# A third product of each gate and value group in blocks of 128, and GpSimd for the weights' sums behind the last scores

## The chip, the core and the metric

The kernel runs on one core of one Trainium2 chip. The time is that of the device for one execution, in microseconds (us), and the figure that counts is the median of the runs. TensorE (PE) does the matmuls, VectorE (DVE), ScalarE (ACT) and GpSimd (POOL) work elementwise, SyncE (SP) issues the transfers. SBUF is the memory on the chip that all engines read, PSUM the banks that matmuls write.

## What is computed

Attention with a threshold, and behind it a feed-forward block with a gate, all in f32. B, H, S, D = 8, 8, 576, 64; the block has 4608 tokens, width 512 and an inner width of 1536.

```python
scores = q @ k.T / sqrt(D)
scores = where(scores >= max(scores) - 0.02, scores, -1e9)
attn = softmax(scores) @ v                      # (B, H, S, D)
x = attn.transpose(0, 2, 1, 3).reshape(4608, 512)
g = x @ w_gate                                  # 512 -> 1536
out = (g * sigmoid(g) * (x @ w_val)) @ w_out    # 1536 -> 512
```

## The kernel before

**Stages.** After the loads and the first batch, scores and attention of the next batches run slot by slot, and the feed-forward products of earlier batches are put between them. The tokens are cut into chunks c = 0 to 8: eight of 512 tokens, one per batch, and chunk 8 with the last 64 tokens of all eight batches. Behind the last scores, from `tail[0] = True` (L1996) on, chunks 7 and 8 are left, with no scores beside them. This stretch is called the tail here.

**Gate and value products.** A chunk needs, for 256 columns of the inner width at a time (a group, g = 0 to 5), the gate and the value of both halves of 256 tokens (t = 0, 1). A Strassen scheme does this by seven products of operand sums in place of eight; each is four matmuls with a 128x128 weight and 256 tokens. The products are p1 to p7, and results are sums of several of them. Class `Group` does it; it accumulates p1 and p2 in bank a (line L993, tile pa), p6, p7 and p4 in bank b (pb), and p5 and p3 in bank e (pe). PE's order is p1 of a group, then p4 of the group before it (L1073, called from L1872), then p5, p2, p6, p3, p7. ACT copies bank a into b ahead of p6 (L1000), copies half of b out after p6 (L1037) and after p7 (L1068).

**Gating.** `Group.finish` (L1041) does it for one half t: ACT's tanh (L1045), DVE's (tanh + 1) x value with the value read from PSUM (L1046, "value factor" in what follows), and a multiplication by the gate, by POOL (line L846) in the slots and by DVE (line L849) in the tail. L846 and L849 are the helpers for every tensor_tensor of POOL and of DVE. Half t = 0 reads the value from bank a and is done after p3, half t = 1 from bank b after p4. The result lies in tile hall.

**The tail's groups.** There `LateGroup` (L1145) does p5 and p3 "nested": each product of 256 blocks is split again into seven products of 128x128 with 128 tokens (L1154), which fill seven quarters of two banks (tiles pe and sc). They need operand sums of their own: of the tokens, four sums of 128x256 per chunk by DVE (`deepen_x`, L1104), and of the weights, four of 128x256 per group by DVE (`deepen_weights` and `four_sums`, L1136 and L1096), made for the next group as soon as its weights have landed. After the product four operations join the quarters (`four_quarters`, L1120): for p5 from copies that ACT puts into SBUF (L1166, L1167), for p3 from PSUM, with one quarter copied by ACT (L1126). L1184 (g1) then adds p3's result to the half gate of t = 0; an L849 adds p5's result for t = 1 (g2).

**Output products.** `Deep` (L1399) does those of a chunk, hall times w_out, again by seven products, and each of them by seven blocks of 128. Its operand sums of 128x384 (`inner_sums`) and of 128x512 (`sum`) are DVE's in the tail. The sums for its first product are put in line during group 4 (L1879), the next ones behind p4 of group 4 (`early`), the rest at the end. Its first product stands ahead of the last group's p4 (`gates_end`), its second behind it.

**Order of the work.** PE's order is written out by hand. That of DVE, ACT, POOL and SP is made by class `Plan` (L28) while the program is built: every job has an assumed duration, its dependencies and a rank; the planner goes along in assumed time and gives each engine the ready job of the lowest rank, with a little patience for rank 0. `pe` puts PE's work at its place and forces what it depends on to be planned first. What the planner has fixed is the order of instructions in each engine's queue; on the chip an instruction waits for those ahead of it in its queue.

**Weights.** From chunk 2 on the weights' sums of each group are read from a store in HBM (sums_hbm) into one of two places, as a part of 1 MB (weights of p1, p2, p5, p6) and one of 768 KB (p4, p3, p7); the second is issued when the group that had the place before is through with p4.

## Time and profile before

| | us |
|---|---|
| median of three runs | 1373.76 (1372.51, 1373.76, 1375.14) |
| the profiled execution, its own time | 1371.38 |
| its span, first to last instruction | 1369.2 |
| what lies around the span | 2.2 |
| PE, DVE, ACT, POOL busy | 1351.0, 1070.9, 875.5, 719.9 |
| the first product of chunk 7, start of the tail | 1156.34 |
| the first product of chunk 8 | 1261.02 |
| the end of the last matmul | 1365.57 |
| POOL's last instruction ends | 1143.2 |

The granted clock of TensorE was 1.000 of full speed over the span. The profiled execution lies 2.4 us below the median of the runs. In the timeline's lines the columns are the start, the time from it to the end, engine, line, operation, output tile, input tiles, shapes and how many instructions the line joins; several matmuls joined in one line end when the last of them is out of the array, so lines overlap by a fraction of a microsecond, and the distance of starts is what a product costs. A bracket at the end is the idle time before it and what ended that. In the groups' lines, the busy sum in us and the mean of one in ns stand behind the first bar, and the idle time before them behind the second.

### The profile page before, as it was taken

The numbers are of one execution on the slowest core, as the hardware profiler recorded it, in microseconds if no ns is written. First come the engines' busy times: TensorE is split into PE (matmuls) and PEld (weight loads), VectorE is DVE, ScalarE is ACT, GpSimd is POOL, SyncE is SP. The second block draws the span as 40 slices with busy tenths as digits, with TensorE's granted clock in tenths as the row PEclk, the third lists the DMA queues.
The fourth block names the chain that finished last, engine by engine and source line by source line (L and its number), as shares of the span: only waits on it lengthen the run. The fifth ranks groups of instructions, "written<-read, shape, count | busy, mean of one in ns | idle before, by whom it ended". The sixth has DMA issues, their size and how long they took to land.

```text
span 1369.2 us, 39187 instructions
## 1 busy us (share of the span) xinstructions
PE 1351.0 (99%) x15590; PEld 1116.1 (82%) x15590; DVE 1070.9 (78%) x2815; ACT 875.5 (64%) x2277; POOL 719.9 (53%) x665
## 2 busy tenths in 40 slices
PE   8999999999999999999999999999999999999998
PEld 7777787778788788877887888877887788999998
DVE  7878888887887777777778777777777776787786
ACT  6888776666756766677776766776767764330330
POOL 2688598663564669434973387427943593000000
PEclk9999999999999999999999999999999999999999
DMA  8752424545525540654154513553165403524411
GB/s 177 200 185 90 82 60 133 146 121 156 151 52 155 144 98 27 181 159 117 37 171 128 150 36 128 144 144 87 36 192 144 113 19 143 162 78 146 151 66 32
DMA packets 208294, 162.32 MB, mean 119 GB/s; under 512 B 166128, under 2 KB 180464, under 8 KB 202736
## 3 DMA queue, kind: packets, MB, share of 16 engines
q1 hardware_dynamic: 203920, 158.86, 41.3%
q8 instruction: 124, 2.03, 0.6%
q10 hardware_dynamic: 4192, 0.95, 0.3%
q14 instruction: 58, 0.48, 0.1%
HBM read 138.28 MB, written 21.50 MB: 117 GB/s over the span
## 4 chain that ended last, share of the span: by engine, by line
PE 90%; DVE 3%; DMA 2%; POOL 2%; SPq 1%; issue 1%; ACT 1%; ACTq 0%; DVEq 0%; POOLq 0%
PE pb L993 18%; PE pa L993 12%; PE px L1473 12%; PE sc L1705 10%; PE pe L993 9%; PE xa L1802 9%; PE po L1269 5%; PE py L1482 5%; PE sc L1154 2%; PE pg L1200 2%; PE pv L1200 2%; PE pe L1154 1%; SPq L367 1%; DMA wo<-in_moe_w_val_dram 1%; PE sc L1473 1%
## 5 line engine op out<-in xcount | busy, mean ns | idle before, releaser
L1753 DVE SCALAR_TENSOR_TENSOR pall<-sc,th,pall 128x288 f32<-128x288 f32 x504 | 244.0, 514 | 65.1 <-ACT pall L1751 50.7
L993 PE MATMUL pb<-xall,big 128*128 128x256 f32 x1152 | 273.5, 380 | 0.0
L1751 ACT ACTIVATE pall<-sc,nm 128x288 f32<-128x288 f32 x504 | 232.2, 498 | 34.1 <-DVE pall L1753 33.8
L993 PEld LDWEIGHTS pb<-xall,big 128*128 128x128 f32 x1152 | 216.4, 190 | 31.0 <-issue 2.2
L1781 DVE STREAM_TRANSPOSE pall<-pall 128x576 f32<-128x576 f32 x252 | 189.7, 765 | 58.2 <-ACT pall L1779 41.4
L1779 ACT ACTIVATE pall<-pall,ri 128x288 f32<-128x288 f32 x415 | 189.8, 529 | 26.3 <-DVE ri L1767 25.8
L846 POOL TENSOR_TENSOR hall<-hall,tmp 128x512 f32<-128x512 f32 x80 | 102.3, 1279 | 159.3 <-DVE hall L1046 141.9
L993 PE MATMUL pa<-xall,big 128*128 128x256 f32 x768 | 183.4, 382 | 0.0
L993 PEld LDWEIGHTS pa<-xall,big 128*128 128x128 f32 x768 | 143.0, 190 | 22.2 <-issue 2.7
L1705 PE MATMUL sc<-kT,qT 64*32 64x144 f32 (+1 forms) x5376 | 150.0, 345 | 2.9 <-DVE pall L1753 1.7
L1726 DVE TENSOR_REDUCE mx<-sc 128x2 f32<-128x576 f32 x168 | 124.8, 743 | 28.6 <-PE sc L1705 28.1
L1705 PEld LDWEIGHTS sc<-kT,qT 64*32 64x32 f32 x5376 | 97.8, 106 | 56.9 <-issue 21.0
L993 PE MATMUL pe<-xall,big 128*128 128x256 f32 x576 | 137.2, 381 | 0.4 <-issue 0.4
L1802 PE MATMUL xa<-pall,vall 64*32 64x288 f32 x4032 | 133.0, 404 | 0.9 <-DVE hall L1046 0.8
L1776 POOL TENSOR_SCALAR pall<-pall,ri 128x288 f32<-128x288 f32 x89 | 88.9, 1010 | 67.0 <-DVE ri L1767 63.8
L993 PEld LDWEIGHTS pe<-xall,big 128*128 128x128 f32 x576 | 108.5, 190 | 17.3 <-issue 2.8
L1802 PEld LDWEIGHTS xa<-pall,vall 64*32 64x32 f32 x4032 | 76.5, 107 | 50.6 <-issue 7.4
L1761 ACT COPY sums<-sums 32x6 f32<-32x6 f32 x336 | 66.8, 199 | 45.6 <-DVE pall L1753 41.1
L1045 ACT ACTIVATE vall<-tmp 128x512 f32<-128x512 f32 x96 | 60.2, 630 | 24.6 <-DVE tmp L1058 9.0
L1482 PE MATMUL py<-wo,hall 128*128 128x256 f32 x336 | 74.8, 379 | 0.0
L1728 DVE TENSOR_REDUCE mx<-sc 128x1 f32<-128x288 f32 x168 | 74.8, 445 | 0.0
L846 POOL TENSOR_TENSOR tmp<-tmp 128x512 f32<-128x512 f32 x36 | 45.9, 1276 | 53.4 <-ACT tmp L1068 53.4
(258 smaller groups left out, 2481.3 us busy)
## 6 DMA issues: line engine op xcount, KB each, us to landing
big<-sums_hbm SPq DMA_DIRECT2D x42, 1024.0 KB, 5.4
big<-sums_hbm SPq DMA_DIRECT2D x48, 768.0 KB, 4.7
vall<-in_v_dram SPq DMA_DIRECT2D x112, 144.0 KB, 3.0
out_dram<-big SPq DMA_DIRECT2D x32, 256.0 KB, 3.0
qT<-in_q_dram SPq DMA_DIRECT2D x112, 72.0 KB, 4.8
kT<-in_k_dram SPq DMA_DIRECT2D x112, 72.0 KB, 3.0
wo<-in_moe_w_gate_dram SPq DMA_DIRECT2D x16, 384.0 KB, 4.1
wo<-in_moe_w_val_dram SPq DMA_DIRECT2D x16, 384.0 KB, 4.8
```

The source lines that it names most:

```text
L846: return lambda: nc.gpsimd.tensor_tensor(out=out, in0=a, in1=b, op=op)
L993: nc.tensor.matmul(ps[:, i], w[:, k_, i * P:(i + 1) * P], x[:, k_, :], start=first and i == k_ == 0, stop=True, skip_group_check=True)
L1473: nc.tensor.matmul(ps, a[:, f, :], ws[n][:, f, :], start=bank_ not in begun, stop=True, skip_group_check=True)
L1482: nc.tensor.matmul(ps(), a[:, f, i * P:(i + 1) * P], operands[o][:, f, :], start=first and f == 0, stop=True, skip_group_check=True)
L1705: nc.tensor.matmul(pss[h][(slice(g * G, (g + 1) * G), *part)], qT[hs, col:col + G], kT[hs, c * SH + keys[0]:c * SH + keys[1]], start=True, ...
L1726: rs.append(job("DVE", 0.72, lambda n=n, tile_=tile_: nc.vector.tensor_reduce(out=mx[:, n:n + 2, 0], in_=tile_[:, :, 0:SH], axis=AX.X, op= ...
L1751: ej = job("ACT", 0.42, lambda x=x, n=n: nc.scalar.activation(ps[x], scs[x], AF.Exp, bias=nm[:, n:n + 1]), ej, *((masks[h, 0], masks[h, 1] ...
L1753: masks[x] = job("DVE", 0.45, lambda x=x, n=n: nc.vector.scalar_tensor_tensor(out=ps[x], in0=scs[x], scalar=th[:, n:n + 1], in1=ps[x], op0 ...
L1776: scaled.append(job("POOL", 1.02, lambda x=x, n=n: nc.gpsimd.tensor_scalar(out=x, in0=x, scalar1=ri[:, n:n + 1], scalar2=None, op0=ALU.mul ...
L1779: scaled.append(job("ACT", 0.46, lambda x=x, n=n: nc.scalar.activation(x, x, AF.Copy, scale=ri[:, n:n + 1]), rj, rank=rank))
L1781: seg["turned"].append(job("DVE", 0.72, lambda both=both: nc.vector.transpose(out=both, in_=both), *scaled, rank=rank))
L1802: nc.tensor.matmul(holds[a].ap()[x * G:(x + 1) * G, 0:SH].rearrange("d (i q) -> d i q", q=G), vr[rs, h, j, ds], p[rs, h, :, j, :], start=( ...
```

## The change

In the tail p4 is done nested, as p5 and p3 are. It writes into two fresh banks rather than onto bank b; ACT copies one quarter, DVE joins the quarters from PSUM, adds bank b (new line L1214), and the value factor of t = 1 then reads its value from SBUF. The weights' sums for the nested products pass from DVE to POOL, and four of 128x128 for p4's weights are added, in turn with the other four. The tokens get four more sums of 128x128 by DVE. The gating multiplication of half t = 0 goes from DVE to POOL, but for group 5. The four sums of 128x384 for product 6 of `Deep` go from DVE to POOL. The lines behind the first edit are shifted by up to 31 in the changed kernel.

```diff
...
-        def finish(self, t, gb, gj, hold, mv):
+        def finish(self, t, gb, gj, hold, mv, y=None):
             n, old = turn_of(n_bufs)
             ht = hall[:, t, self.g]
             rank = 0
             tj = job("ACT", 0.55, lambda: nc.scalar.activation(n.ap, gb.ap, AF.Tanh), gj, *old, rank=rank)
-            vj = job("DVE", 0.7, lambda: nc.vector.scalar_tensor_tensor(out=ht, in0=n.ap, scalar=1.0, in1=hold.rows(), op0=ALU.add,
-                                                                       op1=ALU.mult), tj, mv, rank=rank)
+            vj = job("DVE", 0.7, lambda: nc.vector.scalar_tensor_tensor(out=ht, in0=n.ap, scalar=1.0, in1=hold.rows() if y is None else y,
+                                                                       op0=ALU.add, op1=ALU.mult), tj, mv, rank=rank)
             n.jobs = [vj]
-            hold.read_by(vj)
-            hold.done(True)
-            tt, eng, took = (dve_tt, "DVE", 0.62) if tail[0] else (pool_tt, "POOL", 1.3)
+            if y is None:
+                hold.read_by(vj)
+                hold.done(True)
+            else:
+                e_jobs[0] = [vj]
+            tt, eng, took = (dve_tt, "DVE", 0.62) if tail[0] and (t or self.g == NF2 - 1) else (pool_tt, "POOL", 1.3)
             gated[self.c, t, self.g] = mj = job(eng, took, tt(ht, ht, gb.ap, ALU.mult), vj, rank=rank)
             gb.jobs = [mj]
...
+    w4_places = [x[:, 0:3 * P].rearrange("p (n q) -> p n q", q=P) for x in (tall[:, 4 * HW:], vends.rearrange("p a q -> p (a q)"))]
...
-    def four_sums(places, a11, a12, a21, a22, *deps):
+    def four_sums(took, places, a11, a12, a21, a22, *deps):
 
         p1, p2, p3, p4 = places
-        j1 = job("DVE", 0.36, dve_tt(p1, a21, a22, ALU.add), *deps, rank=1)
-        j2 = job("DVE", 0.36, dve_tt(p2, p1, a11, ALU.subtract), j1, rank=1)
-        j4 = job("DVE", 0.36, dve_tt(p4, a12, p2, ALU.subtract), j2, rank=1)
-        return [j4, job("DVE", 0.36, dve_tt(p3, a11, a21, ALU.subtract), j4, rank=1)]
+        j = job("POOL", took, pool_tt(p1, a21, a22, ALU.add), *deps, rank=1)
+        j = job("POOL", took, pool_tt(p2, p1, a11, ALU.subtract), j, rank=1)
+        j = job("POOL", took, pool_tt(p4, a12, p2, ALU.subtract), j, rank=1)
+        return job("POOL", took, pool_tt(p3, a11, a21, ALU.subtract), j, rank=1)
 
     def deepen_x(c, *deps):
 
         if "t" not in x_deep:
-            x_deep["t"] = [qkp.tile([P, S], F32, name=name)[:, 0:2 * HW // 2].rearrange("p (n o q) -> p n o q", n=2, q=P)
-                           for name in ("qT", "kT")]
-        t12, t34 = x_deep["t"]
+            x_deep["t"] = [qkp.tile([P, S], F32, name=name)[:, 0:HW].rearrange("p (n o q) -> p n o q", n=2, q=P) for name in ("qT", "kT", "qT")]
+        t12, t34, last4 = x_deep["t"]
         x = xall[:, 3 * XW:3 * XW + 3 * HW].rearrange("p (o k n) -> p o k n", o=3, k=2)[:, 0:3:2]
         b11, b12, b21, b22 = (x[:, :, k_, n * P:(n + 1) * P] for k_ in range(2) for n in range(2))
         t1, t2, t3, t4 = t12[:, 0], t12[:, 1], t34[:, 0], t34[:, 1]
-        deps = *ready_x[c][1], *ready_x[c][4], *deps
-        j = job("DVE", 0.36, dve_tt(t1, b12, b11, ALU.subtract), *deps, rank=1)
+        mine = *ready_x[c][1], *ready_x[c][4], *deps
+        j = job("DVE", 0.36, dve_tt(t1, b12, b11, ALU.subtract), *mine, rank=1)
         j = job("DVE", 0.36, dve_tt(t2, b22, t1, ALU.subtract), j, rank=1)
         j = job("DVE", 0.36, dve_tt(t4, b21, t2, ALU.subtract), j, rank=1)
         j = job("DVE", 0.36, dve_tt(t3, b22, b12, ALU.subtract), j, rank=1)
-        x_deep[c] = [j], [(b11[:, o], b21[:, o], b22[:, o], t4[:, o], t1[:, o], t2[:, o], t3[:, o]) for o in range(2)]
+        c11, c12, c21, c22 = (x_block(c, 1, 1)[:, k_, n * P:(n + 1) * P] for k_ in range(2) for n in range(2))
+        u1, u2, u3, u4 = (last4[:, n, o] for n in range(2) for o in range(2))
+        i = job("DVE", 0.23, dve_tt(u1, c12, c11, ALU.subtract), *ready_x[c][0], *deps, rank=2)
+        i = job("DVE", 0.23, dve_tt(u2, c22, u1, ALU.subtract), i, rank=2)
+        i = job("DVE", 0.23, dve_tt(u4, c21, u2, ALU.subtract), i, rank=2)
+        i = job("DVE", 0.23, dve_tt(u3, c22, c12, ALU.subtract), i, rank=2)
+        x_deep[c] = [([j], (b11[:, o], b21[:, o], b22[:, o], t4[:, o], t1[:, o], t2[:, o], t3[:, o])) for o in range(2)]
+        x_deep[c].append(([i], (c11, c21, c22, u4, u1, u2, u3)))
 
     def four_quarters(place, q0, q1, one, *deps, psum=False):
...
 
     def deepen_weights(c, g):
 
-        w = flow[:, g % 2 * GW:(g % 2 + 1) * GW].rearrange("p (o k f) -> p o k f", o=NQ, k=2)[:, 2:6:3]
+        parts_ = flow[:, g % 2 * GW:(g % 2 + 1) * GW].rearrange("p (o k f) -> p o k f", o=NQ, k=2)
+        w, v = parts_[:, 2:6:3], parts_[:, 4]
         a11, a12, a21, a22 = (w[:, :, k_, i * P:(i + 1) * P] for i in range(2) for k_ in range(2))
-        places = [w_place[:, g % 2, n] for n in range(4)]
-        ready = four_sums(places, a11, a12, a21, a22, loads[c, g, 0], loads[c, g, 1], *w_users[g % 2], plan.t + plan.PIPE)
-        s1, s2, s3, s4 = places
-        late_sums[c, g] = ready, [(a11[:, o], a12[:, o], s4[:, o], a22[:, o], s1[:, o], s2[:, o], s3[:, o]) for o in range(2)]
+        v11, v12, v21, v22 = (v[:, k_, i * P:(i + 1) * P] for i in range(2) for k_ in range(2))
+        deps = *w_users[g % 2], plan.t + plan.PIPE
+        s1, s2, s3, s4 = places = [w_place[:, g % 2, n] for n in range(4)]
+        j = four_sums(0.75, places, a11, a12, a21, a22, loads[c, g, 0], loads[c, g, 1], *deps)
+        late_sums[c, g] = [([j], (a11[:, o], a12[:, o], s4[:, o], a22[:, o], s1[:, o], s2[:, o], s3[:, o])) for o in range(2)]
+        u1, u2, u4 = (w4_places[g % 2][:, n] for n in range(3))
+        j = four_sums(0.44, (u1, u2, v21, u4), v11, v12, v21, v22, loads[c, g, 1], *deps)
+        late_sums[c, g].append(([j], (v11, v12, u4, v22, u1, u2, v21)))
 
     class LateGroup(Group):
-        def nested(self, o, first, *deps):
+        def nested(self, o, holds, first, *deps):
-            sums, wd = late_sums[self.c, self.g]
-            ready, xd = x_deep[self.c]
+            sums, wd = late_sums[self.c, self.g][o]
+            ready, xd = x_deep[self.c][o]
 
             def fn():
                 for n in ORDER:
                     b_, at_ = AT[n]
-                    nc.tensor.matmul(self.es[b_].ap()[:, at_ * P:(at_ + 1) * P], wd[o][n], xd[o][n], start=b_ not in begun, stop=True,
+                    nc.tensor.matmul(holds[b_].ap()[:, at_ * P:(at_ + 1) * P], wd[n], xd[n], start=b_ not in begun, stop=True,
                                      skip_group_check=True)
...
         def p5(self):
-            m = self.nested(0, True, *(d for h in self.es for d in h.deps))
+            m = self.nested(0, self.es, True, *(d for h in self.es for d in h.deps))
...
         def p3(self):
-            m = self.nested(1, False, *self.c5, *ready_x[self.c][4])
+            m = self.nested(1, self.es, False, *self.c5, *ready_x[self.c][4])
             w_users[self.g % 2] = [plan.t + plan.PIPE]
             y = e_place[:, 0:DM].rearrange("p (f n) -> p f n", n=TC)
             j = four_quarters(e_place, self.es[0].ap(), self.es[1].ap()[:, 0:3 * P], None, m, *e_jobs[0], psum=True)
...
                      j, self.u1, rank=0)
             e_jobs[0] = [g1]
             self.finish(0, u, g1, self.a, self.m2)
+
+        def p4(self):
+            fs = [take("pf") for _ in range(2)]
+            m = self.nested(2, fs, True, *(d for h in fs for d in h.deps))
+            w_users[self.g % 2] = [plan.t + plan.PIPE]
+            j = four_quarters(e_place, fs[0].ap(), fs[1].ap()[:, 0:3 * P], None, m, *e_jobs[0], psum=True)
+            for h, full in zip(fs, (True, False)):
+                h.read_by(j)
+                h.done(full)
+            b, y = self.b, e_place[:, 0:DM].rearrange("p (f n) -> p f n", n=TC)
+            j = job("DVE", 0.7, lambda: nc.vector.tensor_tensor(out=y, in0=b.rows(), in1=y, op=ALU.add), j, rank=0)
+            b.read_by(j)
+            b.done(True)
+            self.finish(1, self.u2_buf, self.g2, None, j, y)
+            if self.g + 2 < NF2:
+                load_flow(self.c, self.g + 2, 1, m)
 
     def plain_group(t, g, n_bufs):
...
             j3 = [self.sum(self.s3, self.a11, self.a21, ALU.subtract, x, self.ready["a11"][x], gated[c, 1, x], mark) for x in range(n)]
             self.ready["s3"] = j3
             self.ready["s1"] = [self.sum(self.a21, self.a21, self.a22, ALU.add, x, j3[x], gated[c, 1, n + x]) for x in range(n - 1)]
-            self.inner_sums(6, self.s3, free_place, j3)
+            self.inner_sums(6, self.s3, free_place, j3, pooled=True)
 
         def late(self, mark):
             c, n = self.c, NF2 // 2
...
             self.ready["s2"] = [self.sum(self.s2, self.a22, self.s3, ALU.subtract, x, j3[x], gated[c, 1, n + x], mark, rank=1) for x in range(n)]
             self.inner_sums(5, self.s2, self.place, self.ready["s2"], self.m1)
 
-        def sum(self, out, a, b, op, x, *deps, rank=2):
+        def sum(self, out, a, b, op, x, *deps, rank=2, pooled=False):
             fs = slice(2 * x, 2 * x + 2)
-            tt, eng, took = (dve_tt, "DVE", 0.62) if tail[0] else (pool_tt, "POOL", 1.3)
+            tt, eng, took = (dve_tt, "DVE", 0.62) if tail[0] and not pooled else (pool_tt, "POOL", 1.3)
             return job(eng, took, tt(out[:, fs], a[:, fs], b[:, fs], op), *deps, rank=rank)
 
-        def inner_sums(self, o, a, place, ready, *deps):
+        def inner_sums(self, o, a, place, ready, *deps, pooled=False):
...
-            tt, eng, took = (dve_tt, "DVE", 0.49) if tail[0] else (pool_tt, "POOL", 1.0)
+            tt, eng, took = (dve_tt, "DVE", 0.49) if tail[0] and not pooled else (pool_tt, "POOL", 1.0)
```

More of the change, by code (lines that the diff above doesn't have):

```diff
@@ L1084 @@
     AT = {0: (0, 0), 1: (0, 1), 5: (0, 2), 2: (0, 3), 3: (1, 0), 4: (1, 1), 6: (1, 2)}
+    tall = tmp.rearrange("p a f n -> p (a f n)")
     end_ = SPARE + P + NF2 * TC
@@ L1394 @@
     u_list, n_list = list(u_bufs), list(n_bufs)
-    tall = tmp.rearrange("p a f n -> p (a f n)")
     CW = NQ * P
```

## Prediction, made before the changed kernel ran

> **What bounds the kernel now.** I read the page's busy shares and slices first, then the chain that ended last, then the timelines of TensorE (PE), VectorE (DVE) and GpSimd (POOL) over the tail, which is the stretch behind the last scores.
>
> ```profile
> PE 1351.0 (99%) x15590; PEld 1116.1 (82%) x15590; DVE 1070.9 (78%) x2815; ACT 875.5 (64%) x2277; POOL 719.9 (53%) x665
> ...
> POOL 2688598663564669434973387427943593000000
> ...
> PE 90%; DVE 3%; DMA 2%; POOL 2%; SPq 1%; issue 1%; ACT 1%; ACTq 0%; DVEq 0%; POOLq 0%
> ```
>
> The reader is to see two things: PE is the bound nearly everywhere, and POOL does nothing in the last six slices, each 34 us long. That idle POOL is what the change spends. The tail runs from 1156.34 us, the first product of chunk 7, to PE's end at 1365.57. In it the waits of PE sum to one of 0.2 us, at 1158.74, for DVE's sums of the tokens. So the tail is worth what its matmuls take. Here is one gate and value group of it, PE's timeline:
>
> ```profile
> 1190.20 1.89 PE L993 MATMUL pa<-xall,big 128*128 128x256 f32 x8
> 1191.93 1.89 PE L993 MATMUL pb<-xall,big 128*128 128x256 f32 x8
> 1193.66 0.61 PE L1154 MATMUL pe<-xall,big 128*128 128x128 f32 x4
> ...
> 1195.22 1.89 PE L993 MATMUL pa<-xall,big 128*128 128x256 f32 x8
> ```
>
> The starts follow each other without a hole. A plain product (p1 at 1190.20, p4 at 1191.93) costs 1.73 us, a nested one (p5, from 1193.66 to 1195.22) 1.56. A group is five plain and two nested products, 11.76 us.
>
> **The change, part by part. The gain.** p4 becomes nested: 1.728 - 1.563 = 0.165 us less, in 2 chunks of 6 groups: 12 x 0.165 = 2.0 us. If the one wait of 0.2 goes too, 2.2 us, 0.16% of the time, is all that PE can give. Everything else in the change can only hold or cost, as PE already has no other gap.
>
> **What is moved to POOL.** Per group eight operand sums: the four of 128x256 that DVE did, and four of 128x128 for p4, and the gating of one half. Their prices:
>
> ```profile
> L846 POOL TENSOR_TENSOR hall<-hall,tmp 128x512 f32<-128x512 f32 x80 | 102.3, 1279 | 159.3 <-DVE hall L1046 141.9
> ...
> L846 POOL TENSOR_TENSOR big<-big,vall 128x256 f32<-128x256 f32 x10 | 7.3, 729 | 0.8
> ...
> L846 POOL TENSOR_TENSOR big<-big,vall 128x128 f32<-128x128 f32 x5 | 2.3, 455 | 0.4
> ```
>
> 4 x 0.73 + 4 x 0.46 + 1.28 = 6.0 us of POOL in a group of 11.6: room enough. The sums' weights land about 8 us after the group's p1 (before: DVE's first of them waits for a DMA until 1279.06 in a group begun at 1271.05), so alone they are done at 7.9 + 4.75 = 12.7. p5 of the next group first needs them at 11.6 + 3.29 + 0.67 = 15.6. Cover 2.9 us. The four sums of 128x384 for Deep's product 6 (4 x 1.0 us) have more than 10 us to their product. SP's issues keep their order; p4's load of the next weights hangs on p4's end as before.
>
> **What DVE and ACT get.** DVE loses four sums (1.68 us) and a gating (0.69), gains four quarters from PSUM (1.55), an addition (0.69), and 0.13 more for the value factor at worst: about the same load. ACT gains a copy of 0.27. The result of p4 is now there later: p4' ends at 3.29, copy, four quarters (1.7), addition (0.7), value factor, gating end near 7.5 instead of 5.2. With the orders of both kernels I walked a group through by these durations. Nothing on PE waits, except that Deep's second product in chunk 7 stands 0.55 us for the addition of group 5, whose bank it needs. Added waits: p4 no longer waits for ACT's copy of p7, but for two fresh banks, long free. Four DVE operations of 128x128 in the tokens' sums (4 x 0.29) are last in rank and hidden under the group before, except ahead of chunk 7. **If DVE and POOL run as fast side by side as alone**, the change gives 2.2 - 0.55 = 1.65 us, up to 2.2.
>
> **But they do not run so side by side.** This decides my forecast. In before's tail POOL is idle, so nothing there shows it. Where both work on two operands in SBUF is in the loading stage; DVE's and POOL's timelines:
>
> ```profile
> 113.97 0.98 DVE L324 SCALAR_TENSOR_TENSOR wo<-hall,wo 128x768 uint32<-128x768 uint32 x1
> 114.88 2.02 DVE L324 SCALAR_TENSOR_TENSOR wo<-xall,wo 128x768 uint32<-128x768 uint32 x1
> ...
> 120.55 0.95 DVE L324 SCALAR_TENSOR_TENSOR wo<-extra,wo 128x768 uint32<-128x768 uint32 x1
> ```
>
> ```profile
> 74.60 1.27 POOL L586 TENSOR_TENSOR hall<-hall,tmp 128x512 f32<-128x512 f32 x1
> ...
> 114.11 1.98 POOL L586 TENSOR_TENSOR hall<-hall,tmp 128x512 f32<-128x512 f32 x1
> 116.05 2.53 POOL L334 TENSOR_TENSOR wo<-wo,big 128x768 uint32<-128x768 uint32 x1
> ```
>
> The two take turns. POOL's operation of 114.11 ends 1.14 us after DVE's first one (114.95), DVE's second ends 0.81 after POOL's (116.09), and POOL's next ends 1.68 after DVE's (the line's shortest, 1.80). Each stands until the other's is over and then needs its own time less some 0.13. Operations of DVE with one operand in PSUM are not drawn out: L1046, a value factor read from PSUM, takes 0.69 in the attention stage, with POOL busy, as in the tail. I take it that f32 tensor_tensors of DVE behave as these; bounds: no effect at all, or full turns.
>
> The Trainium skill, "SBUF — State Buffer", section "Who interferes with whom", says the same as a rule: a VectorE instruction with two inputs in SBUF and a GpSimd one that reads SBUF exclude each other until the first is done, and one input at most in SBUF frees VectorE of it. It speaks against this change, which puts POOL's work beside just such operations; by it the sum is that of full turns, below.
>
> **The turns, priced.** With 0.13 off: POOL 0.60 (128x256) and 0.33 (128x128), DVE 0.30, 0.43 (128x384), 0.57 (128x512). In most groups the four quarters of p5 (SBUF, 0.34 each) meet POOL's sums and end 1 to 2 us later; cover is there. Where it is not is between groups 4 and 5 of each chunk. There DVE has three sums of Deep's first product (128x384) in line ahead of the quarters of p3. Before, two of them stand there, and PE goes on as the last line shows:
>
> ```profile
> 1211.78 1.02 DVE L849 TENSOR_TENSOR big<-hall 128x384 f32<-128x384 f32 x2
> 1212.72 0.41 DVE L849 TENSOR_TENSOR pall<-pall,pe 128x256 f32<-128x256 f32 x1
> ...
> 1215.79 0.69 DVE L1046 SCALAR_TENSOR_TENSOR hall<-vall,pa 128x512 f32<-128x512 f32 x1
> ```
>
> ```profile
> 1217.18 0.61 PE L1154 MATMUL pe<-xall,big 128*128 128x128 f32 x4
> ```
>
> L1046 frees bank a at 1216.48, and p5 of group 5 takes that bank at 1217.18: slack 0.7. In the changed kernel, from group 4's p1: quarters of p5 from 7.5; four of them in turn with POOL's sums 2 x (0.30 + 0.60) + 2 x (0.30 + 0.33) = 3.1, to 10.6; three of Deep's sums with the rest, 3 x 0.43 + 2 x 0.60 + 0.33 = 2.8, to 13.4; then p3's quarters, 1.7, and by the row above 3.1 from their start to L1046, 0.7 for it, and some 0.4 as g1 meets POOL's last sum: 17.6. p5 is due at 14.89. **Stall 2.8**, in two chunks 5.6. Without turns it is 14.4, no stall.
>
> The rest of the full turns: p4' of group 5 then waits for the value factor, 0.6 x 2 = 1.2; Deep's second product in chunk 7 waits 2.3 for the addition; three groups where p5's banks wait for ACT's copy behind a late tanh, 0.45 x 3 = 1.35; the start of chunk 7, where POOL's first eight sums meet the tokens' sums on DVE, 0 to 1.0. Sum 5.6 + 1.2 + 2.3 + 1.35 + 1.0 = 11.45. The low end, no turn but those of POOL's sums with p5's quarters at group 5 and the wait that is there without turns: 2 x 0.6 + 0.55 = 1.75. I take three quarters of the full one, 8.6, since the rows show full turns but between longer operations, and short ones will now and then slip through between two of the other engine's: 8.6 - 2.2 = **+6.4 us**. On the profiled execution's 1371.4 (span 1369.2, 2.2 around it) that is 1377.8; this execution lies 2.4 under the median 1373.76 of the runs, so 1380.2 for a median.
>
> **Rivals.** *First, the other side: cover absorbs the turns.* For it: POOL has 5.6 us idle in each group and 2.9 us cover, DVE's load does not grow, and a stall of PE gives time to everything behind it. It decides if bank a is free at group 5 before 14.9, that is if Deep's three sums and p3's quarters slip by under 0.5 us. Then 1.65 to 2.2 us are gained: 1371.6 to 1372.1, not slower. 0.2% (2.75 us) is about what a measurement can tell from no change, so this counts as the same. *Second, POOL's sums become the bound.* If each of the eight stands for a DVE operation (0.3 to 0.57, say 0.45), they take 3.6 more than 4.75, over the cover of 2.9 by 0.7, at ten p5s: 7 - 2.0 = +5, 1378.8. Against it: DVE idles, or works from PSUM, in a third of that stretch. *Third, small stalls alone*, the low end: 1.75 - 2.2 = -0.4, 1373.3.
>
> **Chances.** Forecast 0.47, absorbed 0.33, POOL's sums 0.11, small stalls 0.09. Slower by over 0.2%: 0.47 + 0.11 and little else, 0.57; within: 0.33 + 0.09, less 0.02 for a gain that the spread of runs lifts over 2.75: 0.40; faster: that 0.02 and 0.01 for a gain that I have not seen, 0.03. Both signs hold much of the chance. The forecast's own range is 1376.5 (5 us of stalls, 2.2 gained) to 1385 (13.5). The range goes down to the absorbed case, 1371.4, and up to full turns, 1373.76 + 11.45 - 2.2 = 1383 and 2 for what a stall pushes on: 1385.
>
> **What would show it.** Right: in the tail of the changed kernel POOL's tensor_tensors of 128x256 and 128x512 have means well above 729 and 1279 ns, DVE's with two SBUF inputs above their 0.42 and 0.69, and PE idles at p5 of group 5 in both chunks, released by DVE's value factor from bank a. The nested p4 at 1.56 us shows the gain. Wrong: means as alone, or drawn out and PE still without gaps (first rival); PE waiting at p5 for POOL (second). A p4 that costs over 1.56, or a wait of p4 for its banks, would fell the gain itself.

## The result and the profile after

The changed kernel takes 1382.28 us (median of 4 runs, 1380.99 to 1385.71) against 1373.29 of the kernel before in runs beside it: ratio 1.0075, 95% interval 1.0061 to 1.0090, 9.0 us more by the medians, 10.3 by the ratio. The forecast was 1380.2, slower, within 1371.4 to 1385. The profiled execution took 1380.99, its span 1379.0. What lies ahead of the tail moves by some microseconds from one execution to the next (the first product of chunk 7 began at 1154.96 here, at 1156.34 before, and between 1155.0 and 1160.7 in the profiles below), so a sharper measure is used beside the ratios: the **tail**, from the start of that product to the start of the last output product. It was 1360.21 - 1156.34 = 203.87 us before and is 1369.96 - 1154.96 = 215.00 now, 11.1 more.

The same lines of the page as before, busy shares, POOL's slices and the chain:

```profile
PE 1353.3 (98%) x15662; PEld 1118.9 (81%) x15662; DVE 1091.2 (79%) x2817; ACT 877.2 (64%) x2289; POOL 813.6 (59%) x779
...
POOL 2788598653556579435953497438843794543450
...
PE 87%; DVE 5%; POOL 2%; SPq 1%; DMA 1%; ACT 1%; issue 1%; ACTq 0%; DVEq 0%; POOLq 0%
```

POOL now works in the tail, and the chain that ended last goes less through PE (87% for 90) and more through DVE (5% for 3). The waits of PE in the tail, which were one of 0.2 us, are these (waiting line, what it waited for, sum in us, times, longest):

```profile
PE pe L1170 <- DVE hall L1046: 4.6, 2, 3.0
PE pa L993 <- ACT pb L1000: 1.8, 1, 1.8
PE sc L1170 <- ACT sc L1000: 1.0, 2, 0.6
PE sc L993 <- ACT tmp L1037: 0.8, 3, 0.3
PE sc L1504 <- DVE pall L1214: 0.8, 1, 0.8
```

9.0 us in all, half of it where the prediction put it: p5 of group 5 (L1170) waiting for the value factor (L1046) that frees bank a, 3.02 us in chunk 7 and 1.56 in chunk 8. No wait in the list is for POOL, so POOL's sums did not become the bound (the second rival), and PE has gaps, so the turns were not absorbed (the first). The gain is there too. Group 4 of chunk 7, PE's timeline:

```profile
1203.34 1.89 PE L993 MATMUL pa<-xall,big 128*128 128x256 f32 x8
1205.07 0.61 PE L1170 MATMUL sc<-xall,big 128*128 128x128 f32 x4
...
1206.63 0.61 PE L1170 MATMUL pe<-xall,big 128*128 128x128 f32 x4
...
1208.19 1.03 PE L993 MATMUL pa<-xall,big 128*128 128x256 f32 x4
```

p4, nested, goes from 1205.07 to 1206.63, 1.56 us; from p1 to p2 it is 4.85 us, where it was 5.02 (1190.20 to 1195.22).

Why bank a is late shows in DVE's groups over the tail (the mean of one in ns is the number behind the comma):

```profile
L849 DVE TENSOR_TENSOR pall<-pall,sc 128x256 f32<-128x256 f32 x47 | 19.8, 420 | 11.6 <-ACT pall L1137 7.6 <-PE sc L993 2.7
L849 DVE TENSOR_TENSOR big<-big,vall 128x256 f32<-128x256 f32 x24 | 15.1, 627 | 1.7
L849 DVE TENSOR_TENSOR hall<-hall,tmp 128x512 f32<-128x512 f32 x14 | 12.4, 889 | 0.4
```

and in POOL's:

```profile
L846 POOL TENSOR_TENSOR pall<-big 128x256 f32<-128x256 f32 x24 | 20.1, 838 | 36.4 <-DMA big<-sums_hbm 22.7 <-PE xa L1833 8.6 <-PE pa L993 2.8
```

The quarters of p5 (big from big and vall, both in SBUF) went from 425 to 627 ns, gating on DVE from 692 to 889. The quarters of p3 and p4 (one operand in tile sc, PSUM) stay at 420. POOL's sums of 128x256 take 838 where 729 was the row; its gatings of 128x512 hardly grew, 1320 for 1279. These are the turns, and here they are in time, first DVE, then POOL, then PE:

```profile
1213.24 2.09 DVE L849 TENSOR_TENSOR big<-big,vall 128x256 f32<-128x256 f32 x3
1215.25 1.80 DVE L849 TENSOR_TENSOR big<-hall 128x384 f32<-128x384 f32 x2
1217.09 0.70 DVE L849 TENSOR_TENSOR big<-big,hall 128x384 f32<-128x384 f32 x1
1217.71 0.41 DVE L849 TENSOR_TENSOR pall<-pall,pe 128x256 f32<-128x256 f32 x1
...
1220.77 0.69 DVE L1046 SCALAR_TENSOR_TENSOR hall<-vall,pa 128x512 f32<-128x512 f32 x1
```

```profile
1213.68 0.63 POOL L846 TENSOR_TENSOR vends<-vends,big 128x128 f32<-128x128 f32 x1
1214.28 0.77 POOL L846 TENSOR_TENSOR pall<-big,pall 128x256 f32<-128x256 f32 x1
1215.01 0.63 POOL L846 TENSOR_TENSOR vends<-big,vends 128x128 f32<-128x128 f32 x1
1215.61 1.03 POOL L846 TENSOR_TENSOR pall<-big 128x256 f32<-128x256 f32 x1
```

```profile
1218.19 0.39 PE L1170 MATMUL pf<-xall,tmp 128*128 128x128 f32 x2
1221.60 1.19 PE L1170 MATMUL pe<-xall,big 128*128 128x128 f32 x4 [3.02 <-DVE hall L1046]
...
1224.72 1.91 PE L993 MATMUL pa<-xall,big 128*128 128x256 f32 x8
```

Three quarters take 2.09 us (1.21 before) and two of Deep's sums 1.80 (1.02 before), POOL's operations lying between them. p3's quarters begin at 1217.71, 14.4 us behind the group's p1 (the walk had 13.4), and L1046 ends at 1221.46, 18.1 behind it (17.6). The same lines show something that the prediction did not have: p5, 1.56 us elsewhere, took from 1221.60 to 1224.72, 3.12. Two windows tell why (busy us and count of PE, PE's weight loads, DVE, ACT and POOL, then the granted clock):

```profile
1217.93:1221.34 3.41, 0.65 (x6) 0.45 (x5) 3.18 (x7) 1.24 (x3) 0.00 (x0) 1.00 0.00 0
1221.34:1224.75 3.41, 3.15 (x15) 3.18 (x16) 3.31 (x6) 0.68 (x2) 1.52 (x1) 0.50 0.00 0
```

Towards the end of the wait of 3.02 us the clock of TensorE went to half, for 3.41 us, and that cost p5 1.56 us more.

### The profile page after: what moved, and what is told of

Same layout as the page of the kernel before. It is cut to its first block, busy times and chain, and to the rows that moved or that the text cites. A ratio compares the mean times of both kernels' runs of the same rounds, so it can differ in the third digit from the quotient of the medians.

```text
span 1379.0 us, 39516 instructions
## 1 busy us (share of the span) xinstructions
PE 1353.3 (98%) x15662; PEld 1118.9 (81%) x15662; DVE 1091.2 (79%) x2817; ACT 877.2 (64%) x2289; POOL 813.6 (59%) x779
## 4 chain that ended last, share of the span: by engine, by line
PE 87%; DVE 5%; POOL 2%; SPq 1%; DMA 1%; ACT 1%; issue 1%; ACTq 0%; DVEq 0%; POOLq 0%
PE pb L993 15%; PE pa L993 12%; PE px L1504 11%; PE sc L1736 10%; PE pe L993 9%; PE xa L1833 9%; PE po L1301 5%; PE py L1513 5%; PE sc L1170 2%; PE pg L1232 2%; PE pv L1232 2%; PE pe L1170 2%; PE sc L1504 1%; PE sc L993 1%; SPq L367 1%
## 5 line engine op out<-in xcount | busy, mean ns | idle before, releaser
L846 POOL TENSOR_TENSOR hall<-hall,tmp 128x512 f32<-128x512 f32 x90 | 115.6, 1284 | 198.8 <-DVE hall L1046 172.9
L993 PE MATMUL pb<-xall,big 128*128 128x256 f32 x944 | 224.4, 380 | 0.0
L993 PEld LDWEIGHTS pb<-xall,big 128*128 128x128 f32 x944 | 177.5, 190 | 26.1 <-issue 2.2
L993 PE MATMUL pa<-xall,big 128*128 128x256 f32 x768 | 183.6, 382 | 1.8 <-ACT pb L1000 1.8
L993 PEld LDWEIGHTS pa<-xall,big 128*128 128x128 f32 x768 | 143.1, 190 | 24.2 <-issue 3.1
L993 PE MATMUL pe<-xall,big 128*128 128x256 f32 x576 | 137.2, 381 | 0.1
L993 PEld LDWEIGHTS pe<-xall,big 128*128 128x128 f32 x576 | 108.5, 190 | 17.0 <-issue 2.5
L846 POOL TENSOR_TENSOR big<-big 128x384 f32<-128x384 f32 (+3 forms) x82 | 82.4, 1009 | 22.8 <-DVE big L849 13.2
```

The source lines that it names most:

```text
L846: return lambda: nc.gpsimd.tensor_tensor(out=out, in0=a, in1=b, op=op)
L993: nc.tensor.matmul(ps[:, i], w[:, k_, i * P:(i + 1) * P], x[:, k_, :], start=first and i == k_ == 0, stop=True, skip_group_check=True)
```

## The experiments

Two theories stood against each other. **Turns**: DVE's operations with two operands in SBUF and POOL's reads exclude each other, so that work given to POOL delays DVE where it has no room. **The chain**: nested p4 makes DVE's own work longer, and POOL is innocent. A third came in on the way, **the banks**. Each ratio is against the kernel before, run on the same chip beside it (its medians there 1370.4 to 1371.3, and 1373.29 for the changed kernel), with the 95% interval. The waits are those of the profile's list, which leaves out the one of 0.2 us of the kernel before.

| run | ratio | interval | PE's waits in the tail, us | tail against before, us |
|---|---|---|---|---|
| changed kernel | 1.0075 | 1.0061 to 1.0090 | 9.0 | +11.1 |
| dead_reads | 1.0038 | 1.0024 to 1.0051 | 3.0 | +3.8 |
| dead_writes | 0.9999 | 0.9990 to 1.0007 | 0 | 0.0 |
| sums_alone | 1.0012 | 1.0002 to 1.0023 | 0.8 | +0.9 |
| no_sums | 1.0178 | 1.0164 to 1.0192 | 17.9 | +25.0 |
| no_sums_pool | 1.0041 | 1.0024 to 1.0057 | 5.4 | +5.6 |
| x_late | 1.0080 | 1.0064 to 1.0095 | 8.1 | +10.2 |
| first_pooled | 1.0044 | 1.0031 to 1.0057 | 5.8 | +6.9 |
| pooled_late | 1.0032 | 1.0020 to 1.0044 | 4.0 | +4.9 |
| banks_apart | 0.9995 | 0.9983 to 1.0007 | 0.9 | -0.7 |
| gating_back | 1.0082 | 1.0065 to 1.0099 | 10.8 | +11.3 |
| banks_alone | 1.0036 | 1.0023 to 1.0049 | 5.4 | +4.8 |
| banks_py | 0.9998 | 0.9987 to 1.0009 | 0.6 | -1.3 |

### Is POOL's reading enough? (dead_reads, dead_writes)

```diff
 # kernel before, deepen_weights; dead_reads:
+        for (x, y), (v1, v2) in zip(...):      # four pairs of the landed weights
+            d = job("POOL", 0.75, pool_tt(dead2, x, y, ALU.add), loads[c, g, 0], loads[c, g, 1], plan.t + plan.PIPE, d, rank=1)
+            d = job("POOL", 0.44, pool_tt(dead1, v1, v2, ALU.add), loads[c, g, 1], d, rank=1)
 # dead_writes, in place of it:
+        d = job("POOL", 0.1, pool_tt(dead[:, 0:1], a21[:, 0, 0:1], a22[:, 0, 0:1], ALU.add), ...)
+        for _ in range(12):
+            d = job("POOL", 0.4, lambda: nc.gpsimd.memset(dead, 0.0), d, rank=1)
```

> The kernel before, with nested products and all its own work as it was, and in each group of the tail POOL does besides eight tensor_tensors (four 128x256, four 128x128) on the landed weights, into a place that nothing reads; extra work, the output is the reference's. Theory (turns: DVE's operations with two inputs in SBUF and POOL's reads exclude each other): DVE's L849 of 128x256 on SBUF operands rise from 0.42 to about 0.6, those with one operand in PSUM stay at 0.42, PE waits at p5 of group 5, released by L1046, and the time rises by 3 to 9 us. Rival (the longer chain of a nested p4 on DVE, or the wait for POOL's results, costs the time): nothing waits for these results and p4 is plain, so within 1 us of before.

> As the run before this one, but POOL's extra work is twelve memsets of 128x384 a group, some 5 us, that read nothing, behind one tensor_tensor of one column that waits for the weights; extra work only. Theory (turns over reads of SBUF): DVE's means stay at 0.42 and 0.69, time within 1 us of before. Rival (any work of POOL slows DVE or the chip): as much slower as with the reads.

The pair is clean: the same kernel, with work on POOL that nobody waits for. With reads the time rises by 0.38% (some 5 us), with writes by nothing. DVE's weight sums over the tail, dead_reads first, then dead_writes:

```profile
L849 DVE TENSOR_TENSOR pall<-big 128x256 f32<-128x256 f32 x24 | 15.6, 651 | 5.4 <-DMA big<-sums_hbm 3.9 <-PE xa L1810 1.5
...
L849 DVE TENSOR_TENSOR pall<-pall,sc 128x256 f32<-128x256 f32 x28 | 11.7, 420 | 1.1 <-ACT pall L1126 0.3
```

```profile
L849 DVE TENSOR_TENSOR pall<-big 128x256 f32<-128x256 f32 x24 | 10.1, 421 | 4.6 <-DMA big<-sums_hbm 3.1 <-PE xa L1806 1.5
```

and what POOL did in the tail of dead_writes:

```profile
L1146 POOL MEMSET vends<- 128x384 f32 x131 | 54.7, 418 | 7.6
```

651 ns with reads, 421 with 54.7 us of memsets, and the sums from PSUM at 420 in both. So the turns are shown, without any dependence and without nested p4. The place was missed: PE did not wait at p5 of group 5 but 2.3 us for the tokens' sums at the start of chunk 7 (tile kT), and 0.7 in Deep. At p5 of group 5 of chunk 7, DVE's and PE's lines in dead_reads are these:

```profile
1219.38 0.69 DVE L1046 SCALAR_TENSOR_TENSOR hall<-vall,pa 128x512 f32<-128x512 f32 x1
```

```profile
1219.03 0.61 PE L1162 MATMUL pe<-xall,big 128*128 128x128 f32 x4
```

L1046 of group 4 ends at 1220.07, and p5 began at 1219.03 without a wait. So with a plain p4, p5 of group 5 does not take the bank that L1046 frees; in the changed kernel, where p4 takes two banks more, it does.

### The sums alone on POOL (sums_alone)

```diff
-        j1 = job("DVE", 0.36, dve_tt(p1, a21, a22, ALU.add), *deps, rank=1)   # and the other three
+        j1 = job("POOL", 0.75, pool_tt(p1, a21, a22, ALU.add), *deps, rank=1)
```

> The kernel before, with only the four weights' sums of 128x256 of each group moved from DVE to POOL; p4 plain, gating and Deep's sums on DVE. Theory (turns): DVE loses 1.7 us of sums a group and gets back up to four waits of 0.6, so about nothing is won: -0.5 to +4 us. Rival (POOL is a free engine, the cost is that of nested p4): DVE is relieved, PE was the bound, within 1 us or 0.2 us of waits less.

+0.12%, interval 0.02 to 0.23%: to relieve DVE of four sums a group and give them to an idle engine did not help, and cost a little. Both sides of the theory's range held it; the rival's 1 us too, so it tells little.

### Nested p4 without POOL's sums (no_sums, no_sums_pool)

```diff
     def four_sums(took, places, a11, a12, a21, a22, *deps):
+        if made[0] > 3:
+            return deps[0]
+        made[0] += 1
 # no_sums only:
-            self.inner_sums(6, self.s3, free_place, j3, pooled=True)
+            self.inner_sums(6, self.s3, free_place, j3)
-            ... "DVE", 0.62) if tail[0] and (t or self.g == NF2 - 1) else (pool_tt, "POOL", 1.3)
+            ... "DVE", 0.62) if tail[0] else (pool_tt, "POOL", 1.3)
```

> The changed kernel with the weights' sums made only for the first two groups of chunk 7 and those of later groups left out (their places keep old values, so most of the products in the tail are of wrong sums), gating and the sums of Deep's product 6 back on DVE: nested p4 and the longer DVE chain with POOL idle. Theory (turns): PE's waits shrink from 9.0 us to at most 2, the clock stays at 1.0, and nested p4 shows its gain: -2.2 to +0.5 us against before. Rival (the longer chain of nested p4 is the cost): waits stay near 9 us, +6 to +9.

> The changed kernel with the weights' sums made only for the first two groups of chunk 7 and left out for later ones (old values stand in their places, so most products of the tail are of wrong sums); gating of t = 0 and the four sums of Deep's product 6 stay on POOL. Beside the changed kernel it lacks POOL's sums alone. Theory (their turns with DVE make the stalls at p5 of group 5): those stalls fall from 3.0 and 1.6 to at most 0.5, the clock stays at 1.0 there, and Deep has no waits; left are the start of chunk 7 (1.8) and the small ones on ACT (up to 1.8): +0.5 to +3 us against before. Rival (DVE's own load with nested p4 is the cost, as in the run without sums and with gating and inner sums on DVE): waits in group 5 and Deep of more than 4 us in all, +6 or more.

The first was a plain miss: +24 us, with POOL idle but for the sums of the first two groups. Its waits lie nearly all in Deep; here are those of chunk 7, PE's timeline:

```profile
1239.07 0.94 PE L1508 MATMUL sc<-big,hall 128*128 128x128 f32 x6 [1.61 <-DVE pall L1218]
...
1244.76 1.65 PE L1508 MATMUL px<-wo,hall 128*128 128x128 f32 x6 [4.08 <-DVE hall L849]
...
1252.13 0.94 PE L1508 MATMUL px<-big 128*128 128x128 f32 x6 [0.77 <-DVE big L849]
...
1255.08 0.94 PE L1508 MATMUL px<-extra,big 128*128 128x128 f32 x6 [2.01 <-DVE big L849]
```

PE waits for sums that DVE makes in SBUF. From 1210 to 1250 us DVE is 91 to 95% busy in each ten; in the kernel before it was 94 to 97% from 1210 to 1240, with no wait. So in that stretch DVE was already the second bound, and nested p4 makes its queue longer. The order in the queue has a part in it too: the operation that ends the wait of 4.08 us, a 128x384 sum in hall, began at 1244.14 and stands behind eight sums of 128x256 of the next chunk's tokens (tile xall, 1239.66 to 1243.03). The second run, with gating and the sums for product 6 left on POOL, has of these only one, of 2.0 us where none was expected, for the addition of group 5 (L1214 of the changed kernel, L1218 here); all its waits:

```profile
PE sc L1508 <- DVE pall L1218: 2.0, 1, 2.0
PE pa L993 <- ACT pb L1000: 1.8, 1, 1.8
PE sc L993 <- ACT tmp L1037: 0.8, 3, 0.3
PE pe L1174 <- DVE hall L1046: 0.8, 2, 0.6
```

Without POOL's sums the stalls at p5 of group 5 go from 4.6 to 0.8 and the clock stays at 1.0, as the turns say: p5 waits for the same L1046 there, so it is not the choice of the bank that differs. But the whole was +0.41%, not under +3 us: the chain has its share.

### Which of the moves helps (gating_back)

The edit is the gating line of no_sums alone.

> The changed kernel with the gating of t = 0 back on DVE, everything else as changed. Theory (turns and load of DVE both count): POOL's 1.3 us a group met little of DVE's work on two SBUF operands, since POOL waits for L1046 and then works beside reads of PSUM, while DVE has no room between groups 4 and 5 and in Deep: the stall at p5 of group 5 grows to 3.5 to 4.5 and Deep's waits grow by more than 2: +12 to +20 us against before. Rival (less work on POOL means fewer turns): 1 to 3 us less than the changed kernel.

Both were wrong: 1.0082, tail +11.3, the same as the changed kernel within the interval. But its waits are 10.8 us for 9.0 (that for L1214's addition rose from 0.8 to 2.1, the others little), and what hides it is that no stretch at half clock followed its longest wait, 3.17 us, which had cost the changed kernel 1.56. So gating on POOL saves some 1.8 us of waits. What separates no_sums from no_sums_pool, 19 us of tail, is then probably for the most part the four sums for Deep's product 6, and the half clock behind the waits that they cause; that move alone was not run.

### What stands ahead in DVE's queue (x_late, first_pooled, pooled_late)

```diff
-        i = job("DVE", 0.23, dve_tt(u1, c12, c11, ALU.subtract), *ready_x[c][0], *deps, rank=2)
+        i = job("DVE", 0.23, dve_tt(u1, c12, c11, ALU.subtract), *ready_x[c][0], *deps, plan.t + 6.0, rank=2)
 # first_pooled (pooled_late has both):
-            self.inner_sums(0, self.a11, self.place, self.ready["a11"], mark)
+            self.inner_sums(0, self.a11, self.place, self.ready["a11"], mark, pooled=tail[0])
```

> The changed kernel with the tokens' four new sums of 128x128 put off by 6 us in the planner's time, so that in DVE's queue at the start of chunk 7 they stand behind the quarters of the output product of chunk 6, which free the bank that ACT copies into. Theory (three of these sums, drawn out by turns with POOL to 2.0 us, make the wait of 1.8 us at p2 of the first group): this wait falls to 0.3 or less, the rest stays: 1.5 to 2.1 us less than the changed kernel, +7 us against before. Rival (the sums of weights on POOL are late there, or the 256 wide token sums): the wait stays over 1.2.

> The changed kernel with the four sums of 128x384 of Deep's first product on POOL too, so that three of them no longer stand ahead of p3's quarters of group 4 on DVE. Theory: L1046 of group 4 ends 2.5 us earlier (three drawn out sums), the stall at p5 of group 5 falls from 3.0 to 0.7 in chunk 7 and to 0 in chunk 8, and with the long stall the half clock goes (1.5 us): 4 to 6 us less than the changed kernel, +3 to +5 against before. Rival (the stall comes from the chain of p4 and the quarters of p5, not from what stands in line): the stall stays over 2.

> Both of the last two edits: Deep's first sums on POOL and the tokens' new sums put off. Theory: the two gains add up, 6 to 8 us less than the changed kernel, +1 to +3 against before; what is left are small stalls by ACT's copies, less the gain of nested p4. Rival: the stalls move on into Deep, whose sums come later, and less than 4 us are won.

x_late takes the wait of 1.8 at the start of chunk 7 away, as expected, but only 0.9 us of the tail are won, not 1.5 to 2.1: Deep's wait for L1214 went from 0.8 to 1.5, and the ratio is the changed kernel's. In first_pooled p5 of group 5 no longer waits for L1046 in either chunk; its waits, but for 0.7 us on DVE:

```profile
PE sc L1170 <- ACT sc L1000: 2.2, 3, 0.9
PE pa L993 <- ACT pb L1000: 1.8, 1, 1.8
PE sc L993 <- ACT tmp L1037: 1.1, 4, 0.3
```

4.3 us of tail are won, as expected, though more of the work is on POOL and in turns; against before it is still +6.9, not +3 to +5. With three drawn out sums gone from ahead of p3's quarters, L1046 of group 4 ends 16.2 us behind the group's p1, at 1220.40, and not 18.1. That is still behind the start of p5, 1219.30, which did not wait for it: the planner also gave p5 another bank, and there a wait of 0.9 for ACT's L1000. So the run does not part what stands in the queue from the choice of the bank. Both edits together win 6.2 us of tail, within the 6 to 8 expected (+4.9 against before, not +1 to +3). What PE then waits for is, but for 0.7 us, ACT. At p5 it needs nothing of ACT's copy L1000. At p7 it needs L1037, but that copy is itself late: at 1187.35 in pooled_late it begins when p3's last product in tile sc is through, not when p6 is, more than a microsecond before.

### The banks (banks_apart, banks_alone, banks_py)

In the tail the banks of the products are four single ones and four halves of two tiles (sc). The nested p4 takes two more, and so bank b of some groups falls onto a half (the products p6 and p7 of line L993 then write tile sc, which they never did before) whose other half belongs to a nested product. The suspicion was that a wait then comes from the neighbour, the other half of the same tile.

```diff
     def take(name, full=False):
+        if tail[0] and name in ("pa", "pb", "pe", "pf"):
+            free = [b for b in free if (b.fixed is None) == (name in ("pa", "pb")) and (b.full or not full)] or free
+            if name in ("pe", "pf"):
+                return Hold(min(free, key=Bank.free_at), name)
 # banks_py besides (and p4's and p5's two banks always from one tile):
+        if tail[0] and name == "py":
+            return Hold(min((b for b in free if b.fixed is not None), key=Bank.free_at, default=free[0]), name)
```

> The version with Deep's first sums on POOL and the tokens' new sums put off, and besides the tail's groups take banks a and b only from the four single banks, and those of the nested products only from the halves of the two tiles that the scores had (tile sc). Theory: the 3.3 us that PE still waits there for ACT (its copies L1000 and L1037 of the one half, while PE wants or has just written the other half of the same tile) are waits on a neighbour and not on data; they go, with some 0.25 us each of restart: 4 to 5 us less than the version before it, and then -1.5 to +1 us against before. Rival (ACT is late with its copies, whichever bank they are in): the waits stay over 2 us, under another tile's name, and so does the time.

> The changed kernel with the rule for banks alone (banks a and b of the tail's groups from the four single banks, those of nested products from the halves of tile sc); Deep's first sums stay on DVE ahead of p3's quarters, the tokens' new sums where they were, so the turns on DVE and POOL are those of the changed kernel. Theory that the choice of banks is half of the cause: p5 of group 5 no longer takes the bank that L1046 frees, the next copy of a into b (needed by p2, 1.6 us later) does, so the stall of 3.0 falls to 1 to 1.6, the one of 1.6 to nothing, the half clock goes, ACT's small waits go; left are 1.8 at the start of chunk 7 and some in Deep: 0 to +3 us against before. Rival (DVE is too late for any bank): over 3 us of stalls stay in group 5, +5 or more.

> The version with Deep's first sums on POOL, the tokens' sums put off and the banks apart, and in addition the bank of Deep's fifth product from the halves of tile sc, which are idle there, not from the one that ACT still copies. Theory: the wait of 0.7 us for ACT (L1530 there) goes, PE's waits in the tail are 0.3 at most, and what is left is the gain of nested p4: 1.0 to 2.2 us less than before, 0.07 to 0.16%. Rival: another wait takes its place in Deep (the sums of s1, which come at the same time), and it stays at the 0.5 to 0.7 us of the version before it.

banks_apart is pooled_late with this rule: all of ACT's 3.3 us are gone, and the tail is 0.7 us shorter than before's. Its waits:

```profile
PE py L1517 <- ACT pall L1530: 0.7, 1, 0.7
PE py L1517 <- DVE hall L853: 0.2, 1, 0.2
```

The rule alone, on the changed kernel, goes half the way: 1.0036, some +5 us, where 0 to +3 was expected. Its waits but for one of 0.2:

```profile
PE pa L997 <- ACT pb L1004: 3.6, 3, 1.8
PE py L1517 <- DVE big L853: 1.6, 2, 1.4
```

The stall moved from p5 to p2 of group 5, as expected, 0.9 us in each chunk (the third of the first line, 1.8, is at the start of chunk 7), and a new one of 1.4 came in Deep. With the turns as they were, the bank that p5 takes is thus worth about half of the cost. banks_py takes the wait of 0.7 away, and its tail is the shortest of all, 1.3 us under before's:

```profile
PE sc L1528 <- DVE hall L864: 0.6, 1, 0.6
```

Part of what was won came back as a longer wait for the sums of s1, as its rival said. By the runs neither version can be told from the kernel before: 0.9995 (0.9983 to 1.0007) and 0.9998 (0.9987 to 1.0009). No version here beats it beyond the measurement, and the whole gain, 0.15%, is hardly more than half the width of these intervals.

## Why the prediction was right, and where not

- **The gain of 2.0 us.** Right. The nested p4 took 1.56 us. In banks_py it stands nearly alone: -2.0 for the products, -0.2 for the wait of before that went, +0.6 for a wait and some +0.3 for its restart make -1.3, as measured.
- **The turns.** Right, shown by dead_reads against dead_writes, and by means of 627 for 425 ns. The price was a little high: three quarters took 2.09 us, where the walk gives 2.2 to 2.4 for three pairs. That f32 tensor_tensors behave as the operations of the loading stage was assumed, and it is so. The rule of the Trainium skill, "SBUF — State Buffer", section "Who interferes with whom", holds here in both halves, that a read on POOL is needed and that one operand in PSUM frees DVE.
- **The stall at p5 of group 5**, 2.8 twice, three quarters taken, so 4.2: measured 3.0 and 1.6, 4.6. In chunk 7 the full figure was right (the walk's own terms, 17.6 - 14.89, give 2.7); chunk 8 took over the walk of chunk 7 and came to little more than half. That p5 of group 5 takes bank a in the kernel before too, with 0.7 us to spare, was a misreading: dead_reads shows it beginning ahead of L1046's end. The stall needs both, turns that make L1046 late and the two banks of nested p4 that make p5 take its bank; the second was not in the sum, and it is by banks_alone half of the matter.
- **p4 of group 5, 0.6 twice**: not seen. That p5's stall in the same group had given the time fits, but is not shown: in no_sums_pool and first_pooled, where that stall is small or gone, p4 does not wait either.
- **Deep's second product, 2.3**: 0.8. Here p5's stall did give the time: in no_sums_pool, nearly without it, the same wait is 2.0.
- **ACT's copies, 3 x 0.45**: 1.0 and, at L1037, 0.8 that I had not seen. The mechanism was named as a late ACT; it was the neighbour in the same tile, as pooled_late and banks_apart show.
- **The start of chunk 7, 0 to 1.0**: 1.8, and by another way: not POOL's sums were late, but DVE's quarters of the output product, which stood behind the new 128x128 sums "hidden" there. "Except ahead of chunk 7" was the right place, without a price.
- **What the sum lacked.** Its 8.6 us of waits were 9.0, and that this is so near is luck: two terms were too high by 1.8 us in all (p4 of group 5 and Deep), three too low by 2.2. The tail grew by 11.1, though, and the waits and the gain make 9.0 - 0.2 - 2.0 = 6.8. Of the 4.3 left, 1.56 is the half clock; the rest, 2.8 over nine waits, is 0.3 each that the list of waits does not hold (called restart here): the time to the end of the matmul before, and a slower first product (at 1160.23 eight matmuls took 1.83 us for 1.73, and p2 began 1.98 behind its place with a wait of 1.81 listed). Hence 9 us and not 6.4: right in sign and in the turns, a third too small.
- **That DVE's load is about the same**, and so costs nothing, was the weakest step. It is the same on average, but in the stretch of groups 4 and 5 and Deep DVE was 94 to 97% busy before. no_sums shows what a little more does there.

## What to carry to other kernels

An engine that stands idle is not a free one: GpSimd's reads take turns with VectorE's operations on two SBUF operands, so look at what VectorE does in that moment, and at its load in that stretch and not over the span. Where the queue of the second busiest engine is full, what stands ahead of the operation that frees a PSUM bank, and which bank the next product takes, decided more than the amount of work moved: two moves in the queue and two rules for banks took the tail from +11.1 to -1.3 us. And price a stall of TensorE with its restart, 0.3 us here, and, from some 2 us on, with the chance of a clock at half behind it, which cost 1.6 us here.

## What the runs showed of the hardware that was not expected

**The clock.** In all fourteen traces the granted clock changes only at instants that lie whole multiples of 3.413 us apart (in x_late it went to half at 41.15 and at 1222.16 us, 346 times 3.413 later), and within the execution it stays at half for 3.41 or 6.83 us. In the tail a wait halved it when enough of the wait fell between two such instants: in the changed kernel 2.76 of 3.41 us were without a product (first window above). A wait of 3.17 us in gating_back, at the same place, lay across such an instant, with 1.96 and 1.21 us without a product, and the clock stayed at 1.00:

```profile
1223.03:1226.44 3.41, 1.45 (x13) 1.26 (x12) 3.24 (x8) 0.29 (x1) 0.00 (x0) 1.00 0.00 0
1226.44:1229.85 3.41, 2.20 (x17) 2.18 (x18) 3.25 (x7) 1.99 (x5) 0.00 (x0) 1.00 0.00 0
1229.85:1233.26 3.41, 3.41 (x20) 3.05 (x19) 3.24 (x7) 0.87 (x3) 0.00 (x0) 1.00 0.23 72
```

In no_sums one of 2.01 us lay whole between two instants, and half the clock followed:

```profile
1253.08:1256.49 3.41, 1.41 (x9) 1.35 (x10) 3.41 (x10) 0.44 (x1) 0.00 (x0) 1.00 0.16 36
1256.49:1259.90 3.41, 3.41 (x9) 2.66 (x8) 0.55 (x2) 0.53 (x2) 0.00 (x0) 0.50 0.52 195
```

Over the tails of all runs, every stretch at full clock with 1.99 us or more without a product was followed by one at half (five: 2.99 in x_late, 2.76, 2.16, 2.00, 1.99), and none with 1.96 or less. A single wait of 2.96 us in no_sums (1.52 and 1.44) did nothing. In the loading stage, with other products, less was enough (0.91 us in banks_alone, from 117.57), so this is no general bound. The Trainium skill, "TensorE: Matmul & The Clock Gate", section "Part 1: The HAM clock gate", has a free-running window of some 3.4 us for it, and half the clock after an idle one. The 3.413 us of the traces, which do not start with the wait, agree with that window; that a window with 1.99 us without a product was enough does not agree with a whole idle one.

**The neighbour in a tile.** A product or a copy waited for work on the other half of its two-bank tile, 3.3 us of PE's time in pooled_late, and none of it was left when the banks a and b no longer shared a tile with a nested product (banks_apart). The profile shows these as waits for semaphores; whether the memory would ask for them too was not tried.
